# Exact-part value products for the first batch, and a later cut of one block's tokens

## The chip, the core and the metric

The kernel runs on one core of a Trainium2 chip. The core has five engines that work beside each other and are tied by semaphores: TensorE (matmul; PE and PEld in the profile), VectorE (DVE), ScalarE (ACT), GpSimd (POOL) and SyncE (SP), which issues most DMAs. The metric is the device time in microseconds. A time is the median of several executions; a profile is one more execution, recorded instruction by instruction.

## What is computed

An attention with a polynomial sketch, and a SwiGLU feed-forward block on its output. The parts of the reference that matter:

```python
batch, n_heads, seq, head_dim = (4, 4, 1088, 32)     # r = 8
def phi(x):
    a = np.einsum('rd,bhsd->bhsr', S1, x)
    b = np.einsum('rd,bhsd->bhsr', S2, x)
    return np.einsum('bhsi,bhsj->bhsij', a, b).reshape(*x.shape[:-1], r * r)
q_p, k_p = (phi(q), phi(k))
kv = np.einsum('bhsf,bhsd->bhfd', k_p, v)
z = np.sum(k_p, axis=2)
num = np.einsum('bhsf,bhfd->bhsd', q_p, kv)
den = np.einsum('bhsf,bhf->bhs', q_p, z)[..., None] + 1e-06
x = num / den                                        # to (4352, 128)
g = x @ w_gate                                       # d_ff 1536
silu = g * (1.0 / (1.0 + np.exp(-g)))
out = (silu * (x @ w_val)) @ w_out
```

The inputs are float64 and are read as pairs of 32-bit words; the kernel narrows them to float32 itself.

## The kernel before, in words

**Tokens and units.** The 4352 tokens are cut into blocks. Batch 0 (the "first batch", 1088 tokens) is blocks 0, 1 and 2 of 384, 384 and 320 tokens. The rest is seven blocks: 3 to 8 of 480 and 9 of 384. The feed-forward width of 1536 is twelve chunks of 128. A *unit* (i, j) is block i with chunk j: the gate and the value product, silu, and their product, which is one hidden tile in one of a list of `slots`. A *down* product multiplies a hidden tile by a chunk of `wo` and adds it up in a bank of PSUM; after it the slot goes back to the end of the list.

**Two kinds of unit.** `unit` makes both products in float32 (L1015), takes silu on ScalarE (L1019) and multiplies on VectorE straight out of PSUM (L1030). `cut_unit` makes a product from *exact parts*: weights and tokens are each split into a coarse part (w1, x1), a remainder (wb, x0) and a mixed part (wd, xd), each stored as fp32r. One product is then three fp32r matmuls: xd by wd (L968), x1 by w1 (L978) and x0 by wb (L979). ScalarE copies the first out of PSUM (L972), VectorE adds the others to it (L980), and GpSimd multiplies by silu (L991). With `both=False` the gate product stays in float32 (L970); with `both=True` both are made from parts.

**Making parts.** For weights of three chunks: ScalarE makes w1, an engine subtracts (`low`), ScalarE scales it (wb), and the engine makes wd (`cut_weights`, L865). For `wv` the engine is GpSimd, for `wg` VectorE. For tokens of one block (`cut_tokens`): ScalarE makes x1 (L875), GpSimd x0 (L876) and, in a later step, VectorE xd (L880).

**Narrowing.** Each weight piece of three chunks is turned from 64-bit words into float32 by `narrow` in three steps: two masks on VectorE (L256, L257); two activations on ScalarE (L261, L262); two joins on VectorE (L264, L270) and one product on GpSimd (L279).

**Order.** The scheduling is by hand: each engine runs its instructions in the order in which the Python program issues them. In the first-batch loop (L1278) a step z issues one unit of `seq`, then steps of narrowing (`parts`), from z=17 on one down product and one piece of the attention of the next batch (`parts_of`), and between them the parts of `wv`. A `late` unit, of which there are six before the loop, leaves silu and the value product apart, and `catch_up` (L1036) multiplies them on GpSimd later: three ahead of the loop, three at z=24, 25 and 26. After the loop come 23 down products among pieces of the attention, then the main loop over y (84 units of blocks 3 to 9), the first 20 of them with the gate product in float32. In both loops each engine is in order, so an instruction that waits holds up what is behind it.

**The attention of batch 1** runs beside z=17 to 29: kT and qT are transposed on VectorE, key sketches on TensorE (L347), features `phk` on VectorE (L370), sums of features `zs` on GpSimd (L540); then `values` on TensorE: `key_values` (L381) and four products with `zs` (L713), and after them the key sketches of batch 2. `fold` and `spread_out` follow on VectorE (L594 to L723), and the query sketches (L335) need what `fold` writes. `query_step` makes `phT` on VectorE, and `numerators` (L776) uses it. The attention of batch 2 has the same course in the main loop: `values` ahead of y=4, the query sketches ahead of y=6.

**Buffers.** Before, there are 27 slots of 384 columns: 17 in `hbuf` and 10 in `late`. In the main loop `hbuf` is cut anew into 13 slots of 480 columns; `late` holds remainders of the gate weights, later the features of batch 3 and the parts of `wo`. From z=17 on units take turns in three PSUM banks.

The steps z of the first-batch loop and the main loop's y are numbered as in the code; z=12 starts at 41.00 us in the profile, z=18 at 49.38, z=29's unit ends at 76.54, and y=0 starts at 93.06.

Of the kernel before, what the change touches and what calls it, by code (L numbers as in the profile page):

```python
# [19 lines left out]
def kernel(  # L20
# [28 lines left out]
    nc = tc.nc  # L49
# [253 lines left out]
    NH = 27  # L303
    NL = 10
    hbuf = const.tile([P, NH - NL, BW], FP32, name="hbuf")
    late = const.tile([P, NL, BW], FP32, tag="late", name="late", bufs=1)
    slots = [(hbuf[:, k, :] if k < NH - NL else late[:, k - NH + NL, :]) for k in range(NH)]
# [300 lines left out]
    def attentions():  # L608
# [31 lines left out]
        values(kvz[:, 0, :], phk, zs)  # L640
        kab, kcopies = sketched(wide("b"), key_products, 2, "kab2")
        fold(kvz[:, 0, :])
# [23 lines left out]
        for b in (2, 3):  # L666
# [19 lines left out]
            if b == 2:  # L686
                yield from turn_queries(3)
                phk = late[:, NL - 6 :, :].rearrange("p s (n h i j) -> p (s n) h i j", h=1, i=R, j=R)
                phk = phk.rearrange("p (c h) o i j -> p c (h o) i j", h=H)
                yield from features(phk, kab)  # L690
                zs, sums = feature_sums(phk)
# [17 lines left out]
    def values(kv, phk, zs):  # L709

        key_values(kv[:, 0:F], phk, 0, NC)
        for h in range(H):
# [105 lines left out]
    def homes(w):  # L818


        if w is wv:
            for c in range(4):
                yield [
                    stage.tile([P, 3, P], F32R, tag=tag, name=name, bufs=6)[:]
                    for tag, name in (("exp", "w1"), ("man", "wb"), (("exp", "man")[c % 2], "wd"))
                ]
        else:
            big = lambda pool, tag, bufs: pool.tile([P, 2, 3, P], F32R, tag=tag, name="g" + tag, bufs=bufs)
            for c in range(2):
                t = [big(stage, "raw", NRAW), big(stage, "raw", NRAW), big(apool, "phq", 2)]  # L830
                for k in range(2):
                    yield [x[:, k] for x in t]

    def cut_weights(w, lows, engine):

        rows = [], [], [], []
        sub = dict(op=ALU.subtract)
        for c, (w1, wb, wd) in enumerate(homes(w)):
            src = w[:, 3 * c : 3 * c + 3, :]
            low = lows[c]  # L840
            w_parts[id(w), c] = (w1, wb, wd)
            fine = dict(out=wd, in0=whole(w1), in1=whole(wb), **sub), engine.tensor_tensor
            if engine is nc.vector:
                fine = dict(
                    out=wd, in0=low, scalar=-BETA, in1=whole(w1), op0=ALU.mult, op1=ALU.add
                ), engine.scalar_tensor_tensor
            for row, f, args in zip(
                rows,
                (nc.scalar.activation, engine.tensor_tensor, nc.scalar.activation, fine[1]),
                (  # L850
                    dict(out=w1, in_=src, func=AF.Copy, scale=CUT),
                    dict(out=low, in0=src, in1=whole(w1), **sub),
                    dict(out=wb, in_=low, func=AF.Copy, scale=BETA),
                    fine[0],
                ),
            ):
                row.append((f, args))
        return rows

    def take(steps, n):  # L860

        for _ in range(n):
            if steps:
                f, args = steps.pop(0)
                f(**args)  # L865
# [410 lines left out]
    seq += [(i, j) for j0 in (6, 9) for i in range(3) for j in range(j0, j0 + 3)]  # L1276
    order = [(i, j) for i in range(3) for j in range(NCH)]
    for z, (i, j) in enumerate(seq):  # L1278
# [3 lines left out]
        unit(i, j)  # L1282
        for p in parts.get(z, ()):
            part(*p)
        if z in (24, 25, 26):
# [5 lines left out]
        if z >= 17:  # L1291
            todo.remove(order[0])
            todo.insert(0, order.pop(0))
            down()
# [119 lines left out]
```

## Time and profile before

| what | us |
|---|---|
| median of 8 runs (lowest to highest) | 287.17 (286.62 to 288.54) |
| the profiled execution | 286.97 |
| its span, first to last instruction | 285.0 |
| PE busy in 93.06 to 111.06 (18.00) | 16.86 |
| PE busy in 111.06 to 190.00 (78.94) | 78.40 |
| POOL, L991 hidden products x83 | 105.0 |
| DVE, L980 sums x83 | 83.3 |
| ACT, L972 copies x83 | 70.9 |

A span is shorter than the time of its execution by what lies before the first and after the last instruction. A line of a timeline gives start and length in microseconds, engine, line of the code, operation, output and inputs, tile sizes, how often, and in brackets how long the engine had been idle and who ended that. A line of waits gives the waiting engine and line, who released it, the total, how often and the longest. A line of stages gives the stretch, its length, and the busy time of PE, PEld, DVE, ACT and POOL. Lengths of matmuls overlap, so start-to-start times tell their cost. The TensorE clock is 1.00 throughout.

### The profile page before, as it was taken

To read this page: it belongs to the slowest core of one execution; us is meant where nothing else is said; L and a number is where in the kernel's file an instruction comes from. 1 tells how busy PE (TensorE), PEld (TensorE's weight loads), DVE (VectorE), ACT (ScalarE), POOL (GpSimd) and SP (SyncE) were. 2 spreads that over 40 slices of the span, in tenths; PEclk is the share of its full clock that TensorE was granted. 3 is DMA by queue.
4 is the path that set the end of the run, shared out by engine and by line. 5 is a ranking of instruction groups with operands and counts; after the bars stand their busy time and mean duration, and the time that the engine had idled before them with its cause. 6 is when DMAs were issued, how large, how long until landed. Compare 5 with 4: busy or idle time off the path is not lost.

```text
span 285.0 us, 5583 instructions
## 1 busy us (share of the span) xinstructions
PE 277.1 (97%) x2129; PEld 191.3 (67%) x2129; DVE 220.7 (77%) x324; ACT 175.2 (61%) x316; POOL 177.1 (62%) x173
## 2 busy tenths in 40 slices
PE   8899999999999989999999999999999999999995
PEld 7545565666665656555576767657777777778984
DVE  3997988975495968998557898749889969988741
ACT  3567665723401846655366776867878888877760
POOL 3315432279500876589935787759879789878660
PEclk9999999999999999999999999999999999999999
DMA  6574193222311122000200020001000200010021
GB/s 195 160 218 114 55 285 117 81 78 81 92 31 28 26 81 74 21 0 2 33 18 0 0 36 2 0 2 22 13 0 1 37 0 0 10 28 1 0 35 28
DMA packets 26138, 14.28 MB, mean 50 GB/s; under 512 B 19840, under 2 KB 24192, under 8 KB 26112
## 3 DMA queue, kind: packets, MB, share of 16 engines
q1 hardware_dynamic: 25456, 13.84, 18.7%
q8 instruction: 16, 0.26, 0.4%
q10 hardware_dynamic: 656, 0.10, 0.2%
q14 instruction: 10, 0.08, 0.1%
HBM read 11.41 MB, written 2.23 MB: 48 GB/s over the span
## 4 chain that ended last, share of the span: by engine, by line
PE 89%; DVE 5%; ACT 2%; POOL 2%; issue 1%; DVEq 0%; ACTq 0%; POOLq 0%
PE PS L1060 24%; PE PS L1015 16%; PE PS L968 11%; PE PS L978 10%; PE PS L979 10%; PE PS L970 4%; PE PS L776 2%; PE PS L335 2%; PE PS L234 2%; PE PS L347 1%; POOL hbuf L991 1%; PE PS L381 1%; DVE xd L880 1%; PE PS L1088 1%; PE PS L1055 1%
## 5 line engine op out<-in xcount | busy, mean ns | idle before, releaser
L991 POOL TENSOR_TENSOR hbuf<-sg,sum 128x480 f32<-128x480 f32 (+1 forms) x83 | 105.0, 1269 | 37.7 <-ACT sg L986 29.4
L980 DVE SCALAR_TENSOR_TENSOR sum<-PS,sum 128x960 f32<-128x960 f32 (+2 forms) x83 | 83.3, 1003 | 26.7 <-ACT sum L972 21.6
L972 ACT ACTIVATE sum<-PS 128x960 f32<-128x960 f32 (+2 forms) x83 | 70.9, 854 | 39.4 <-PE PS L968 37.9
L1060 PE MATMUL PS<-hbuf,wo 128*128 128x480 f32 (+3 forms) x142 | 57.5, 505 | 0.0
L968 PE MATMUL PS<-xd,gphq 128*128 128x480 f32 (+1 forms) x63 | 40.1, 636 | 0.5 <-DVE xd L880 0.5
L978 PE MATMUL PS<-x,w 128*128 128x480 f32 (+1 forms) x83 | 38.5, 464 | 0.0
L986 ACT ACTIVATE sg<-sum 128x480 f32<-128x480 f32 (+1 forms) x63 | 36.6, 581 | 0.9 <-DVE sum L980 0.9
L968 PE MATMUL PS<-xd,wd 128*128 128x480 f32 (+1 forms) x83 | 35.8, 432 | 0.5 <-DVE xd L880 0.5
L1060 PEld LDWEIGHTS PS<-hbuf,wo 128*128 128x128 f32 x142 | 26.6, 189 | 8.4 <-issue 0.9
L979 PE MATMUL PS<-x,wb 128*128 128x480 f32 (+1 forms) x83 | 31.2, 376 | 0.0
L1015 PE MATMUL PS<-xT,wg 128*128 128x384 f32 (+1 forms) x74 | 29.5, 480 | 0.0
L1015 PE MATMUL PS<-xT,wv 128*128 128x384 f32 (+1 forms) x74 | 28.8, 471 | 0.2 <-DVE wv L279 0.2
L1019 ACT ACTIVATE sg<-PS 128x384 f32<-128x384 f32 (+1 forms) x31 | 14.3, 466 | 21.4 <-PE PS L1015 19.8
L968 PEld LDWEIGHTS PS<-xd,wd 128*128 128x128 f32 x83 | 15.7, 189 | 13.1 <-issue 11.4
L978 PE MATMUL PS<-x,graw 128*128 128x480 f32 (+1 forms) x63 | 23.5, 373 | 0.2 <-ACT xT L793 0.2
L979 PE MATMUL PS<-x,graw 128*128 128x480 f32 (+1 forms) x63 | 23.3, 370 | 0.0
L1060 PE MATMUL PS<-hbuf,scaled 128*128 128x480 f32 x48 | 23.2, 564 | 0.0
L1015 PEld LDWEIGHTS PS<-xT,wv 128*128 128x128 f32 x74 | 13.8, 190 | 9.2 <-DVE hbuf L1030 0.9
L968 PEld LDWEIGHTS PS<-xd,gphq 128*128 128x128 f32 x63 | 11.9, 188 | 11.7 <-issue 6.8
L1015 PEld LDWEIGHTS PS<-xT,wg 128*128 128x128 f32 x74 | 13.3, 189 | 9.3 <-issue 1.2
L978 PEld LDWEIGHTS PS<-x,w 128*128 128x128 f32 x83 | 15.6, 188 | 5.8 <-issue 3.6
L979 PEld LDWEIGHTS PS<-x,wb 128*128 128x128 f32 x83 | 15.6, 188 | 5.7 <-issue 4.3
(173 smaller groups left out, 457.6 us busy)
## 6 DMA issues: line engine op xcount, KB each, us to landing
kld<-in_k_dram SPq DMA_DIRECT2D x4, 544.0 KB, 4.1
vld<-in_v_dram SPq DMA_DIRECT2D x12, 144.0 KB, 4.4
qld<-in_q_dram SPq DMA_DIRECT2D x3, 544.0 KB, 3.4
raw<-in_moe_w_out_dram SPq DMA_DIRECT2D x4, 384.0 KB, 3.8
raw<-in_moe_w_gate_dram SPq DMA_DIRECT2D x3, 384.0 KB, 3.7
raw<-in_moe_w_val_dram SPq DMA_DIRECT2D x3, 384.0 KB, 4.0
out_dram<-o SPq DMA_DIRECT2D x16, 60.0 KB, 1.9
vld<-in_v_dram SPq DMA_DIRECT2D x4, 112.0 KB, 4.3
```

Of the source, the lines that this page charges most:

```text
L234: nc.tensor.matmul(ps[0:32, 0:w], warm[:, 0:32], warm[:, 0:w], start=True, stop=True)
L968: nc.tensor.matmul(ds[:, k], wd, xd, start=True, stop=True)
L970: nc.tensor.matmul(g, wg[:, j, :], xT[:, t0 : t0 + n], start=True, stop=True)
L972: nc.scalar.activation(sums, ds, AF.Copy, scale=-1.0 / BETA)
L978: nc.tensor.matmul(ps[:, k], w1, x1, start=True, stop=False)
L979: nc.tensor.matmul(ps[:, k], wb, x0, start=False, stop=True)
L980: nc.vector.scalar_tensor_tensor(out=sums, in0=ps, scalar=1.0 + 1.0 / BETA, in1=sums, op0=ALU.mult, op1=ALU.add)
L986: nc.scalar.activation(sg, sums[:, 0] if both else g, AF.Silu)
L991: nc.gpsimd.tensor_tensor(out=hj[:, 0:n], in0=sg, in1=sums[:, len(ws) - 1], op=ALU.mult)
L1015: nc.tensor.matmul(o[:, 0:n], w[:, j, :], xT[:, t0 : t0 + n], start=True, stop=True)
L1019: nc.scalar.activation(sg[:, 0:n], g[:, 0:n], AF.Silu)
L1060: nc.tensor.matmul(acc[i][:, 0:n], w, hidden[i, j][:, 0:n], **sides)
```

## The change

It has two parts.

*Part 1.* In the main loop, the parts of block 4 (`line[1]`) are issued in units 3 and 8 instead of 2 and 3: ScalarE's x1 and GpSimd's x0 after y=3, VectorE's xd after y=8. That puts xd behind VectorE's `fold` and `spread` of batch 2's sums and behind five more of the units' sums.

*Part 2.* In the first batch the eighteen units of chunks 6 to 11 are made block by block (all of block 0, then 1, then 2) instead of three chunks at a time. The last twelve of them, z=18 to 29, blocks 1 and 2, become `cut_unit` with the gate in float32 and the value product from parts. For that the parts of `wv` are made in two halves: chunk groups 3 and 2 (chunks 9 to 11 and 6 to 8) at z=11 to 16, groups 0 and 1 at z=20 to 27; tokens of block 1 at z=13 and 15, of block 2 at z=16 and 19. The three late products go from z=24 to 26 to z=8 to 10. In the attention of batch 1 the four products with `zs` move behind the key sketches of batch 2 (`value_sums` apart from `key_values`). There are 24 slots of 384 instead of 27 (14 in `hbuf`, 4 in `late`, 6 in a new tile `more`), 11 slots of 480 in the main loop up to y=20 and 15 from there, instead of 13. The weights' parts get other homes, and `cut_weights` and `take` become a generator `cut_chunk` with the same four instructions.

```diff
-    NH = 27
+    NH = 24
     NL = 10
     hbuf = const.tile([P, NH - NL, BW], FP32, name="hbuf")
-    late = const.tile([P, NL, BW], FP32, tag="late", name="late", bufs=1)
-    slots = [(hbuf[:, k, :] if k < NH - NL else late[:, k - NH + NL, :]) for k in range(NH)]
+    late = const.tile([P, 4, BW], FP32, tag="late", name="late", bufs=1)
+    more = const.tile([P, NL - 4, BW], FP32, name="more")
+    slots = [t[:, k, :] for t, n in ((hbuf, NH - NL), (late, 4), (more, NL - 4)) for k in range(n)]
...
-        values(kvz[:, 0, :], phk, zs)
+        key_values(kvz[:, 0, 0:F], phk, 0, NC)
         kab, kcopies = sketched(wide("b"), key_products, 2, "kab2")
+        value_sums(kvz[:, 0, :], zs)
         fold(kvz[:, 0, :])
...
         if w is wv:
+            x, y = (big(apool, "phq", 2) for _ in range(2))
+            yield 3, [x[:, 0], x[:, 1], y[:, 0]]
+            x = const.tile([P, 3, 3, P], F32R, name="w2")
+            yield 2, [x[:, k] for k in range(3)]
+            yield 0, [exp(), man(), exp()]
+            yield 1, [exp(), man(), man()]
         else:
+            for c in range(NCH // 3):
+                x = big(stage, "raw", NRAW)
+                yield c, [x[:, 0], x[:, 1], (exp, man)[c % 2]()]
...
+    def cut_chunk(w, home, low, engine):
+        c, (w1, wb, wd) = home
+        src = w[:, 3 * c : 3 * c + 3, :]
+        nc.scalar.activation(w1, src, AF.Copy, scale=CUT)
+        yield
+        engine.tensor_tensor(out=low, in0=src, in1=whole(w1), op=ALU.subtract)
+        yield
+        nc.scalar.activation(wb, low, AF.Copy, scale=BETA)
+        yield
...
+            engine.tensor_tensor(out=wd, in0=whole(w1), in1=whole(wb), op=ALU.subtract)
+        w_parts[id(w), c] = w1, wb, wd
+        yield
...
-    seq += [(i, j) for j0 in (6, 9) for i in range(3) for j in range(j0, j0 + 3)]
+    seq += [(i, j) for i in range(3) for j in range(6, NCH)]
...
+        if z == CUTS:
+            turn[0] = 1
+        if z < CUTS:
+            unit(i, j)
+        else:
+            cut_unit(i, j)
...
-        if z in (24, 25, 26):
+        if z in (8, 9, 10):
             catch_up()
...
+        if z == 11:
+            give(cut_chunk(wv, next(home_v), room_for(fpool, "o", 2), nc.gpsimd), 11, 12, 14, 15)
+            give(cut_chunk(wv, next(home_v), room_for(fpool, "o", 2), nc.gpsimd), 12, 13, 15, 16)
+            give(cut_tokens(1), 13, 15)
+            give(cut_tokens(2), 16, 19)
         if z == 20:
+            lows = [room_for(fpool, "o", 2) for _ in range(2)]
+            give(cut_chunk(wv, next(home_v), lows[0], nc.gpsimd), 20, 21, 25, 26)
+            give(cut_chunk(wv, next(home_v), lows[1], nc.gpsimd), 21, 22, 26, 27)
         if z >= 17:
             parts_of(1)
+        for gen in steps_at.get(z, ()):
+            next(gen, None)
...
-        for at in {2: (20, 22), 3: (27, 32), 4: (40, 42)}.get(m, (NCH * m - 10, NCH * m - 9)):
+        for at in {1: (3, 8), 2: (20, 22), 3: (27, 32), 4: (40, 42)}.get(m, (NCH * m - 10, NCH * m - 9)):
...
         if y == GATES:
             hold("g2")
+            slots += wide_slots(more, NL - 4)
```

`CUTS` is 18. The instructions of each engine, in order: up to z=10 as before but for the two catch-up products among them; on GpSimd then the last catch-up product, `low` of chunk groups 3 and 2, x0 of block 1, the product of wo piece 0, wd of group 3, the product of wo piece 1, wd of group 2, x0 of block 2, and from there the hidden products of the units. From y=0 on every engine's order is the one before, apart from the two moved steps of block 4.

## The prediction

> **What bounds the kernel now.** I read the busy shares first, then what TensorE waited for, then the stages, then single engines around the two places that are edited.
>
> ```profile
> PE 277.1 (97%) x2129; PEld 191.3 (67%) x2129; DVE 220.7 (77%) x324; ACT 175.2 (61%) x316; POOL 177.1 (62%) x173
> ```
>
> TensorE works 277.1 of 285.0 us. Its waits, longest in total first:
>
> ```profile
> PE PS L335 <- DVE spread L723: 1.1, 1, 1.1
> PE PS L968 <- DVE xd L880: 1.0, 2, 0.5
> ```
>
> The busy times by stage:
>
> ```profile
> 41.00:49.38 8.38, 8.38 (x27) 4.94 (x26) 6.82 (x17) 4.64 (x11) 2.08 (x3) 1.00 0.52 166
> 49.38:76.54 27.16, 27.16 (x295) 17.95 (x294) 18.04 (x36) 12.19 (x29) 17.70 (x18) 1.00 0.22 69
> ```
>
> After the length the columns are PE, PEld, DVE, ACT and POOL. From 41.00 (step z=12 of the first-batch loop) to 76.54 (end of z=29) TensorE never rests, so work removed there is time gained and any wait added there is time lost. The first stage shows the room that POOL has before z=18: it works 2.08 of 8.38 us. The prices on TensorE, from its timeline (start, length, instruction):
>
> ```profile
> 48.74 0.81 PE L1060 MATMUL PS<-hbuf,wo 128*128 128x384 f32 x2
> 49.38 0.70 PE L1015 MATMUL PS<-xT,wg 128*128 128x320 f32 x2
> 49.92 0.70 PE L1015 MATMUL PS<-xT,wv 128*128 128x320 f32 x2
> ```
> ```profile
> 256.22 0.34 PE L968 MATMUL PS<-xd,wd 128*128 128x384 f32 x1
> 256.39 0.34 PE L978 MATMUL PS<-x,graw 128*128 128x384 f32 x1
> 256.57 0.34 PE L979 MATMUL PS<-x,graw 128*128 128x384 f32 x1
> ```
>
> Starts count, not lengths, since matmuls overlap: a float32 product of 384 columns takes 0.64 us (48.74 to 49.38), one of 320 takes 0.54, a product of exact parts of 384 takes 0.174.
>
> **What the Trainium skill says.** "FP8 and Floating Point Precision", TensorE Precision Notes: true FP32 makes four passes. The trace agrees: 0.64 / 0.174 = 3.7. "SBUF — State Buffer", Who interferes with whom: a VectorE instruction with two SBUF inputs and a GpSimd instruction that reads SBUF exclude each other, and the later one blocks until the first is through. The trace agrees in both directions. On VectorE:
>
> ```profile
> 92.27 0.65 DVE L880 SCALAR_TENSOR_TENSOR xd<-x,x 128x480 fp32r<-128x480 f32 x1
> ...
> 104.29 1.65 DVE L880 SCALAR_TENSOR_TENSOR xd<-x,x 128x480 fp32r<-128x480 f32 x1 [2.27 <-POOL x L876]
> ```
>
> The first met an idle POOL, the second a POOL product from 104.22 to 105.42. On POOL, two hidden-tile products started at 98.90 and 100.08 (1.18 apart), and the next steps, into each of which one such VectorE instruction fell, were 1.49 long: 0.31 each. "Perfetto Trace Analysis", GPSIMD Engine Instruction, advises start-to-start times for GpSimd; they are 0.96 us for a 128x384 product here (26.71, 27.67, 28.62).
>
> **Part 1: the tokens of block 4 in units 3 and 8.** In y=3 VectorE first waits for POOL (2.27 us), then runs xd (1.65), and only then `fold` and `spread` (105.87 to 106.8); TensorE's sketches (L335) wait 1.09 us for that. Moved to y=8, xd leaves `fold` behind the second gate remainder (L865, over at 102.02): s123 is done near 103.1, against 105.76 when TensorE comes. The 1.09 us go. What is late next: ScalarE's copy and POOL's remainder x0 are issued a unit later, behind one more hidden product (1.2 us) with five units to spare. At y=8 xd costs 1.1 us (mean of L880, which includes blocking) to 1.65 where VectorE has no idle time (112 to 122). Queued behind it are the sums of y=9 to 13; that of y=10 started 2 us behind TensorE and would end near 123.2, its bank being reused three units later, near 124. VectorE's small waits from 128 to 134 let it catch up. xd itself is ready near 119.5 and wanted at 121.8. I take -1.0; bounds -1.1 and -0.4 (lost cover at y=10). No DMA moves queue; the shift and load issues of `spread` only go out earlier.
>
> **Part 2: twelve units by exact parts.** The set of shapes from z=18 on is the same before and after (six units of 384, six of 320). *Gain on TensorE:* the value product falls from 0.645 to 3 x 0.174 = 0.522 for 384 (-0.123), from 0.538 to 3 x 0.145 = 0.435 for 320 (-0.103; 0.145 is the 384 step by columns). 6 x 0.123 + 6 x 0.103 = -1.36.
>
> *What ScalarE and VectorE get:* per unit one copy out of PSUM on ScalarE (L972 with 480 columns 0.57) and L980 instead of L1030 on VectorE (0.64 for 480 columns, by columns 0.51 for 384, against 0.55 for L1030: no more). ScalarE worked 12.19 of 27.16 us, so twelve copies of 0.5 fit.
>
> *What POOL gets before z=18.* In program order it now has, after the gate piece at 39.61: three catch-up products (from z=24 to 26 to z=8 to 10), the narrowing of wv piece 4, two `low`, x0 of block 1, wo piece 0, wd of chunk 3, wo piece 1, wd of chunk 2. That wd is the stationary operand of the first matmul of z=18, due at 49.38. From 39.61 these are twelve steps of 0.96: 39.61 + 12 x 0.96 = 51.1, plus 0.1 to pass on. So TensorE stands at least 1.9 us even if nothing blocks. That floor needs no assumption beyond in-order issue. Then the blocking: the same stretch has seven VectorE instructions with two SBUF inputs (L264 and L270 of wv 4, wo 0, wo 1; xd of block 1). At 0.31 each, 7 x 0.31 = 2.2 on POOL. And they come in a chain: L264 of wv 4 (40.60) meets the catch-ups, delaying L270 to about 43.3 and with it wv 4; xd waits for x0 near 48.5, then for POOL's product; L264/L270 of wo 1 come behind xd, and wo 1 behind them, before wd. Walking that queue gives wd of chunk 2 at 54.1 to 54.3, 4.7 us late; with only the 2.2 added, 53.4, 4.0 late. I take 4.4; bounds 1.9 and 5.1. The smaller waits at z=13 and z=17 (late VectorE products, late banks) lie inside it, as TensorE would wait at z=18 anyway.
>
> *What comes after.* From z=18 to `zs` of batch 1 POOL has x0 of block 2 (0.85), seven hidden products (0.96 each; before, z=24's catch-up was the only one), two wo pieces, two `low` and the sums, which took from 62.92 to 68.38:
>
> ```profile
> 62.92 2.49 POOL L540 TENSOR_TENSOR zs<-phk 128x512 f32<-128x512 f32 x2
> 65.49 2.08 POOL L540 TENSOR_TENSOR zs<-zs 128x512 f32<-128x512 f32 x2
> 67.65 0.73 POOL L540 TENSOR_TENSOR zs<-zs,phk 128x256 f32<-128x256 f32 x1
> ```
>
> That is 0.85 + 6.7 + 3.84 + 5.46 = 16.9, plus five blockings (1.6) and some 2.9 idle while the first units are made: 21.4. TensorE reaches `value_sums` after 6 x 1.82 + 3 x 1.62 + 1.28 + 1.13 + 1.22 = 19.4 (units with their down products, first key sketches, values, second key sketches, which the split puts ahead of the sums). Missing: 2.0. Also z=24's exact product needs the one bank that VectorE frees with the sum of z=23, behind three phk products: 0.4 if nothing blocks, up to 1.9 if L264/L270 of wo 3 do; the more is lost there, the less at `zs`. I take +2.3 together; bounds 0.9 and 2.8. At z=28 the DVE chain to phT starts as before; its end (85.2) has 1.3 us before the numerators (86.53), which covers POOL products blocking two or three of its steps (0.3 to 0.5 each).
>
> Slots (14 + 4 + 6 instead of 17 + 10), homes and gate steps keep TensorE's order from y=0 on; cover: the slot taken is freed by a down product that TensorE runs before. Cost nothing; at most one late down, 0.2.
>
> **Sum.** -1.0 - 1.36 + 4.4 + 2.3 = +4.3. On the profiled execution (span 285.0, 286.97 with what lies around it) 291.3; the runs' median 287.17 is 0.2 higher, within their spread (286.62 to 288.54). Forecast 291.2 us.
>
> **Rivals.**
> - *Floor only, 287.7.* POOL's queue is late by its work alone (+1.9) and `zs` by 0.9: -2.36 + 2.8 = +0.4. For it: blocking shows only in a few instructions of this trace. Against: every one that overlaps shows it.
> - *The other side, faster, 285.0.* One mechanism: POOL hands over the wd of chunk 2 in time at z=18, and -2.4 stand (286.97 - 2.4 = 284.6; 285.0 with small waits). It decides if the waits at z=18 and `zs` come to less than 2.4 together. Against: twelve steps of 0.96 from 39.61. For: POOL is only 2.08 us busy in the stage before.
> - *Deeper, 293.2.* The rest of a standing of 4 us turns into a slower TensorE clock: "TensorE: Matmul & The Clock Gate", Part 1, gives half clock after an idle window of about 3.4 us, released after as long, an estimate of up to 1.7 us more; no run here shows it (the clock is 1.00 in all stages). Or the lag outlasts 1.3 us at the numerators.
> - *Part 1 does nothing*: another wait takes L335's place; 292.2, inside the forecast's own range.
>
> **How the numbers follow.** Chances: forecast 0.56 (289.5 to 292.6), floor 0.18, faster 0.08, deeper 0.18. About 0.3% (0.86 us) is what a measurement of this kernel can tell from none. The floor case straddles it (0.08 same, 0.10 slower). So faster 0.08, same 0.08, slower 0.84. Leaving out faster, the lower half of the floor and the top of deeper gives 288.0 to 293.4.
>
> **What would show it.** TensorE idle before the first xd,w product near 49.4, released by POOL's wd, ending near 54 (51.3 for the floor); POOL near full from 40 to 54; L264/L270 near 41 and 47 lengthened from 0.55 to about 1; a wait of the sums (L719) for zs or of L972 for VectorE's sum before z=24; steps of 1.82 us from unit to unit from z=18; no wait of the sketches near y=6. If the first xd,w product starts within 0.5 us of the down product before it, my main term is wrong.

## The result, and the profile after

The kernel after takes 295.74 us (median of 11 runs, 294.89 to 297.29), the one before 287.06 (31 runs, 286.61 to 288.54): 1.0294 times as long, 95% interval 1.0278 to 1.0309. The forecast was 291.2 (288.0 to 293.4). The sign was right, the size a little under half of what came. Of the eleven runs, three kept a mean TensorE clock of 1.000 and took 294.89 to 294.93 us; the other eight, with 0.987 to 0.994, took 295.62 to 297.29, and the profile below is one of these.

The profiled span is 293.9 us. The head of the page (busy time, share, instructions):

```profile
PE 279.3 (95%) x2141; PEld 192.4 (65%) x2141; DVE 227.2 (77%) x326; ACT 181.1 (62%) x330; POOL 191.7 (65%) x187
...
PEclk9999999899999999999999999999999999999999
```

TensorE counts 2.2 us more busy time than before (277.1) though it has less to do. Part of that is the clock, which drops in one slice, the eighth; there the same products take longer. The rest is the way of counting: a product that starts behind a wait doesn't overlap with the one before it (in lows_late, below, the clock stays at 1.00 and the count is still 278.5). What the kernel loses beside the clock is standing still. TensorE's waits, after:

```profile
PE PS L962 <- POOL w L857: 2.8, 1, 2.8
PE PS L972 <- DVE sum L974: 1.7, 2, 1.3
PE PS L962 <- DVE xd L874: 1.0, 2, 0.5
PE PS L719 <- POOL zs L541: 0.9, 1, 0.9
...
PE PS L1009 <- ACT sg L1013: 0.7, 1, 0.7
PE PS L1009 <- DVE more L1024: 0.6, 1, 0.6
PE PS L1009 <- DVE late L1024: 0.6, 1, 0.6
```

L962 is the product xd by wd (L968 before), L972 the first of the two products into the shared bank (978), L1009 the float32 product of `unit` (1015), L719 the product with `zs` (713). All of these but L962's wait for xd (1.0 before too) are new; the sketches' wait of 1.1 us for `spread` is gone. By stages (length; PE, PEld, DVE, ACT, POOL; then the clock):

```profile
41.00:49.40 8.40, 6.48 (x19) 2.86 (x17) 6.38 (x11) 4.25 (x11) 6.64 (x7) 1.00 0.50 163
49.40:55.76 6.36, 3.42 (x10) 1.33 (x8) 5.35 (x10) 2.70 (x7) 4.44 (x6) 1.00 0.00 0
55.76:60.86 5.10, 5.10 (x15) 3.49 (x15) 2.51 (x5) 1.97 (x5) 1.77 (x2) 0.67 0.00 0
60.86:86.71 25.85, 23.28 (x294) 16.67 (x293) 17.79 (x32) 13.84 (x34) 20.52 (x21) 1.00 0.21 69
```

The first row covers the time that z=12 to 17 took before; TensorE now works 6.48 of 8.40 us there, and POOL 6.64 instead of 2.08. z=18's first matmul comes at 55.76 instead of 49.38, and after a standing of 2.8 us the clock is 0.67 for 5.1 us.

The starts of z=12, z=18 and y=0 cut every profile into three stages that can be compared whatever happens ahead of z=12. (It starts between 40.99 and 42.99 us in the profiles below. TensorE's wait for kT near 6 us varies from run to run, up to 1.6 us; in w1_after, banks and combo2 the products right behind it are slower too, 2.0 to 2.2 us for the key sketches of batch 0 instead of 1.49.) In us:

| kernel | z=12 to 18 | z=18 to y=0 | y=0 to end |
|---|---|---|---|
| before | 8.38 | 43.68 | 191.94 |
| after | 14.77 | 47.47 | 190.67 |
| the difference | +6.39 | +3.79 | -1.27 |
| forecast | +4.4 | +0.94 (-1.36 + 2.3) | -1.0 |

So the first two stages hold the error. What holds z=18 up is seen on three engines. Before, the same joins and the product behind them are short, on VectorE and POOL:

```profile
40.60 0.55 DVE L264 SCALAR_TENSOR_TENSOR exp<-raw,exp 128x384 int32<-128x384 int32 x1
41.07 0.55 DVE L270 SCALAR_TENSOR_TENSOR man<-raw,man 128x384 f32<-128x384 uint32 x1
41.70 0.99 POOL L279 TENSOR_TENSOR wv<-man,exp 128x384 f32<-128x384 f32 x1 [1.09 <-DVE man L270]
```

ScalarE after (start, length, instruction, and in brackets the idle time before it and who ended that):

```profile
40.65 0.44 ACT L1013 ACTIVATE sg<-PS 128x320 f32<-128x320 f32 x1 [0.64 <-PE PS L1009]
44.34 0.52 ACT L846 ACTIVATE wphq<-wv 128x384 fp32r<-128x384 f32 x1 [3.26 <-POOL wv L279]
44.77 0.47 ACT L1013 ACTIVATE sg<-PS 128x384 f32<-128x384 f32 x1
```

L846 is w1 of chunk group 3, issued in z=11, so it stands before the silu of z=12. It needs the narrowed piece 4 of `wv`, the silu does not, and ScalarE stands 3.26 us. VectorE after, with the masks (L256, L257) and joins (L264, L270) of the narrowing:

```profile
40.59 1.38 DVE L264 SCALAR_TENSOR_TENSOR exp<-raw,exp 128x384 int32<-128x384 int32 x1
41.89 1.35 DVE L270 SCALAR_TENSOR_TENSOR man<-raw,man 128x384 f32<-128x384 uint32 x1
43.16 0.48 DVE L1024 TENSOR_TENSOR late<-sg,PS 128x320 f32<-128x320 f32 x1
45.28 0.55 DVE L1024 TENSOR_TENSOR more<-sg,PS 128x384 f32<-128x384 f32 x1 [1.64 <-ACT sg L1013]
46.36 1.15 DVE L257 TENSOR_SCALAR man<-raw 128x384 int32<-128x384 int32 x1
48.17 0.35 DVE L257 TENSOR_SCALAR man<-raw 128x384 int32<-128x384 int32 x1
```

And POOL after:

```profile
40.56 2.26 POOL L1030 TENSOR_TENSOR hbuf<-hbuf,sum 128x384 f32<-128x384 f32 x2
43.32 0.99 POOL L279 TENSOR_TENSOR wv<-man,exp 128x384 f32<-128x384 f32 x1 [0.50 <-DVE man L270]
...
48.56 1.00 POOL L870 TENSOR_TENSOR x<-xT,x 128x384 fp32r<-128x384 f32 x1 [1.26 <-ACT x L869]
50.53 1.00 POOL L279 TENSOR_TENSOR wo<-man,exp 128x384 f32<-128x384 f32 x1 [0.96 <-PE PS L1009]
51.49 1.31 POOL L857 TENSOR_TENSOR wphq<-wphq 128x384 fp32r<-128x384 f32 x1
53.76 1.00 POOL L279 TENSOR_TENSOR wo<-man,exp 128x384 f32<-128x384 f32 x1 [0.96 <-DVE man L270]
54.72 0.99 POOL L857 TENSOR_TENSOR w<-w 128x384 fp32r<-128x384 f32 x1
```

Read it as one loop. Two catch-ups on POOL stretch VectorE's two joins (1.38 and 1.35 us; 0.55 alone), so POOL's product for `wv` piece 4 starts at 43.32; ScalarE waits for that, VectorE for ScalarE's silu (1.64), POOL for ScalarE's x1 (1.26) and twice for VectorE's joins (0.96 each; at the first the profile names TensorE, but what the product reads is the join that ended at 50.45). The last line is wd of group 2, for which TensorE stands at z=18. POOL is late not by work alone: from 39.60 to 55.71 its twelve steps take 12.4 us, 0.9 more than 12 x 0.96, and for 3.7 us it stands idle, waiting for engines that it held up itself.

### The profile page after: what moved, and what is told of

Its sections match the earlier page's. It is cut to its first block, busy times and chain, and to the rows that moved or that the text cites. A ratio compares the mean times of both kernels' runs of the same rounds, so it can differ in the third digit from the quotient of the medians.

```text
span 293.9 us, 5655 instructions
## 1 busy us (share of the span) xinstructions
PE 279.3 (95%) x2141; PEld 192.4 (65%) x2141; DVE 227.2 (77%) x326; ACT 181.1 (62%) x330; POOL 191.7 (65%) x187
## 3 DMA queue, kind: packets, MB, share of 16 engines
q1 hardware_dynamic: 25456, 13.84, 18.1%
## 4 chain that ended last, share of the span: by engine, by line
PE 77%; DVE 10%; POOL 5%; DMA 2%; issue 2%; ACT 2%; SPq 0%; DVEq 0%; ACTq 0%; POOLq 0%
PE PS L1054 22%; PE PS L962 11%; PE PS L972 10%; PE PS L973 10%; PE PS L1009 7%; PE PS L964 6%; POOL zs L541 3%; PE PS L782 2%; PE PS L336 2%; DMA kld<-in_k_dram 1%; DVE sum L974 1%; PE PS L348 1%; DVE man L270 1%; DVE man L257 1%; DMA raw<-in_moe_w_out_dram 1%
## 5 line engine op out<-in xcount | busy, mean ns | idle before, releaser
L974 DVE SCALAR_TENSOR_TENSOR sum<-PS,sum 128x960 f32<-128x960 f32 (+4 forms) x95 | 89.4, 941 | 36.5 <-ACT sum L966 21.8
L985 POOL TENSOR_TENSOR hbuf<-sg,sum 128x480 f32<-128x480 f32 (+1 forms) x73 | 91.7, 1261 | 38.1 <-ACT sg L980 24.5
L966 ACT ACTIVATE sum<-PS 128x960 f32<-128x960 f32 (+4 forms) x95 | 76.5, 805 | 52.7 <-PE PS L962 50.8
L1054 PE MATMUL PS<-hbuf,wo 128*128 128x480 f32 (+3 forms) x122 | 50.0, 515 | 0.0
L985 POOL TENSOR_TENSOR more<-sg,sum 128x480 f32<-128x480 f32 (+2 forms) x22 | 25.3, 1152 | 9.1 <-ACT sg L980 5.0
L964 PE MATMUL PS<-xT,wg 128*128 128x480 f32 (+2 forms) x64 | 29.1, 536 | 0.0
L962 PE MATMUL PS<-xd,wexp 128*128 128x480 f32 (+1 forms) x52 | 26.4, 553 | 1.0 <-DVE xd L874 1.0
L1054 PEld LDWEIGHTS PS<-hbuf,wo 128*128 128x128 f32 x122 | 23.0, 191 | 6.2 <-issue 0.4
L962 PE MATMUL PS<-xd,wman 128*128 128x480 f32 (+1 forms) x53 | 27.0, 555 | 0.0
L972 PE MATMUL PS<-x,wraw 128*128 128x480 f32 (+1 forms) x63 | 23.6, 375 | 0.2 <-ACT xT L799 0.2
L973 PE MATMUL PS<-x,wraw 128*128 128x480 f32 (+1 forms) x63 | 23.5, 373 | 0.0
L1009 PE MATMUL PS<-xT,wv 128*128 128x384 f32 (+1 forms) x50 | 20.0, 482 | 1.5 <-DVE more L1024 0.6
L980 ACT ACTIVATE sg<-PS 128x480 f32<-128x480 f32 (+2 forms) x32 | 17.0, 532 | 7.0 <-PE PS L964 6.0
L1009 PE MATMUL PS<-xT,wg 128*128 128x384 f32 (+1 forms) x50 | 20.4, 490 | 0.9 <-ACT sg L1013 0.7
L972 PE MATMUL PS<-x,wexp 128*128 128x480 f32 (+1 forms) x42 | 20.2, 480 | 0.0
L962 PEld LDWEIGHTS PS<-xd,wexp 128*128 128x128 f32 x52 | 9.7, 189 | 10.4 <-issue 7.1
L1054 PE MATMUL PS<-hbuf,scaled 128*128 128x480 f32 x34 | 16.4, 564 | 0.0
L973 PE MATMUL PS<-x,wman 128*128 128x480 f32 (+1 forms) x42 | 15.7, 374 | 0.0
L962 PE MATMUL PS<-xd,w 128*128 128x480 f32 (+2 forms) x27 | 13.0, 481 | 2.8 <-POOL w L857 2.8
L962 PEld LDWEIGHTS PS<-xd,wman 128*128 128x128 f32 x53 | 9.9, 189 | 8.5 <-issue 6.6
```

Of the source, the lines that this page charges most:

```text
L962: nc.tensor.matmul(ds[:, k], wd, xd, start=True, stop=True)
L964: nc.tensor.matmul(g, wg[:, j, :], xT[:, t0 : t0 + n], start=True, stop=True)
L966: nc.scalar.activation(sums, ds, AF.Copy, scale=-1.0 / BETA)
L972: nc.tensor.matmul(ps[:, k], w1, x1, start=True, stop=False)
L973: nc.tensor.matmul(ps[:, k], wb, x0, start=False, stop=True)
L974: nc.vector.scalar_tensor_tensor(out=sums, in0=ps, scalar=1.0 + 1.0 / BETA, in1=sums, op0=ALU.mult, op1=ALU.add)
```

## The experiments

Times are medians; the kernel before beside them took 286.93 to 287.17. Unless a diff says otherwise, the edit is made in the kernel after.

**Each part alone.** `p1_alone`, in the kernel before:

```diff
-        for at in {2: (20, 22), 3: (27, 32), 4: (40, 42)}.get(m, (NCH * m - 10, NCH * m - 9)):
+        for at in {1: (3, 8), 2: (20, 22), 3: (27, 32), 4: (40, 42)}.get(m, (NCH * m - 10, NCH * m - 9)):
```

> The kernel before with only the moved token parts of block 4 (units 3 and 8). My theory: the 1.09 us that TensorE waits for the query sketches ahead of y=6 go and nothing takes their place, so -1.0 to -1.3 us (about 285.9). Rival: xd at y=8, where VectorE has no idle time, delays the sums and gives the gain back: within 0.4 us of before.

`p2_alone` has the opposite edit in the kernel after.

> The changed kernel with the token parts of block 4 back in units 2 and 3. If the two parts add up, it is 1.0 to 1.3 us slower than the changed kernel (about 296.9), and the wait of the query sketches ahead of y=6 is back. Rival: the parts of the first batch have changed the state at y=4, so that the token move is worth less than 0.5 us here.

Part 1 alone: 285.86 us (285.56 to 285.95), ratio 0.9953 (0.9936 to 0.9970), y=0 to the end 190.72. Part 2 alone: 297.14, ratio 1.0348 (1.0314 to 1.0383), y=0 to the end 191.82. The kernel after is 1.4 us faster than part 2 alone, where part 1 alone is worth 1.1: the parts add up within their spread, and part 1 is the whole gain of the third stage.

**When the catch-ups run.** `cu_early`:

```diff
-        if z in (8, 9, 10):
+        if z in (5, 6, 7):
             catch_up()
```

> The changed kernel with its three catch-up products at z=5, 6 and 7, where GpSimd was idle, instead of z=8 to 10. Theory A (a chain: the products delay the narrowing of wv piece 4 on GpSimd, ScalarE's w1 of chunk group 3 waits for that piece and holds up silu, and all later parts are late): ScalarE's wait of 3.3 us falls to below 1.5, TensorE's start of z=18 moves from 55.8 to about 52, the clock stays at 1.00, in all -4 to -5.5 us (290.2 to 291.7). Theory B (only GpSimd's amount of work ahead of z=18 counts): three steps of 0.96 less, z=18 at 52.9, -2.9 us. Theory C (the blocking between VectorE and GpSimd is the main cause and goes wherever the products go): less than -1.5 us.

295.26 us, ratio 1.0285 (1.0242 to 1.0328): z=18 starts 0.53 us earlier (55.23), no more. The stage from z=12 to 18 is 1.66 us shorter (13.11), but TensorE loses 0.93 of that just before z=12, which starts at 42.12. The catch-ups now block other instructions of VectorE, the masks, ahead of the same piece:

```profile
36.12 1.09 DVE L256 TENSOR_SCALAR exp<-raw 128x384 int32<-128x384 int32 x1
37.13 1.15 DVE L257 TENSOR_SCALAR man<-raw 128x384 int32<-128x384 int32 x1
```
```profile
44.09 0.52 ACT L846 ACTIVATE wphq<-wv 128x384 fp32r<-128x384 f32 x1 [2.02 <-POOL wv L279]
```

(VectorE, then ScalarE, of cu_early.) My first theory, that the catch-ups' place makes the lag, fell; the third, that the blocking goes wherever the products go, fits.

**ScalarE's order.** `g3_later` moves all four steps of group 3:

```diff
-            give(cut_chunk(wv, next(home_v), room_for(fpool, "o", 2), nc.gpsimd), 11, 12, 14, 15)
+            give(cut_chunk(wv, next(home_v), room_for(fpool, "o", 2), nc.gpsimd), 14, 15, 17, 18)
```

> The changed kernel with the four steps of chunk group 3 (first needed at z=21) three units later, at z=14, 15, 17 and 18 instead of 11, 12, 14 and 15; nothing else. Theory A (ScalarE's w1 of group 3 stands first in line for wv piece 4 and holds up silu, with it VectorE's products, the masks of wo, the next x1 and so GpSimd): ScalarE's wait for wv piece 4 is gone, wd of group 2 ends near 52 to 53 instead of 55.7, the clock stays at or near 1.00, -3.5 to -5 us (290.7 to 292.2). Theory B (amount of GpSimd work ahead of wd of group 2): one step of 0.96 less, -1 us.

`w1_after` has `12, 12, 14, 15` in that place, which puts one instruction, ScalarE's w1, behind the silu of z=12 and leaves every other engine's order as it was.

> The kernel after, with one instruction moved: ScalarE's w1 of chunk group 3 behind the silu of z=12 instead of ahead of it. Theory A (ScalarE's order holds silu, VectorE's products and so the token parts and GpSimd): silu of z=12 starts near 42.4 instead of 44.77, the wait then falls on the silu of z=13, one unit less deep; z=18's first matmul 0.5 to 1.5 us earlier than 55.76 and the time 294.2 to 295.2. Theory B (GpSimd's own queue sets z=18 whatever ScalarE does): within 0.3 us of 295.7, with only the small waits at z=13 to 17 moved into the one at z=18.

g3_later: 293.59 (ratio 1.0229, 1.0207 to 1.0252), z=12 to 18 in 13.04. w1_after: 294.80 (1.0264, 1.0239 to 1.0290), z=12 to 18 in 13.83. ScalarE of w1_after:

```profile
43.84 0.49 ACT L1013 ACTIVATE sg<-PS 128x384 f32<-128x384 f32 x1 [0.75 <-PE PS L1009]
46.35 0.53 ACT L846 ACTIVATE wphq<-wv 128x384 fp32r<-128x384 f32 x1 [2.03 <-POOL wv L279]
```

z=12 starts at 42.99 in this profile, so its silu now comes 0.85 us after that, instead of 3.78. The standing before w1 shrinks to 2.03 us and meets the next silu. One instruction's place is worth 0.94 us of the stage, the whole group's 1.73. That is theory A in kind, but for g3_later I had put 3.5 to 5 us: the greater part of the 6.39 does not hang on these places.

**All of it moved.** `spread`:

```diff
-        if z in (8, 9, 10):
+        if z in (17, 18, 19):
             catch_up()
...
-        if z == 11:
-            give(cut_chunk(wv, next(home_v), room_for(fpool, "o", 2), nc.gpsimd), 11, 12, 14, 15)
-            give(cut_chunk(wv, next(home_v), room_for(fpool, "o", 2), nc.gpsimd), 12, 13, 15, 16)
-            give(cut_tokens(1), 13, 15)
+        if z == 8:
+            gen3 = cut_chunk(wv, next(home_v), room_for(fpool, "o", 2), nc.gpsimd)
+            give(cut_chunk(wv, next(home_v), room_for(fpool, "o", 2), nc.gpsimd), 8, 9, 11, 12)
+            give(gen3, 13, 14, 16, 17)
+            give(cut_tokens(1), 12, 14)
```

> The changed kernel with all parts that z=18 needs made where GpSimd was idle: group 2 at z=8, 9, 11 and 12 (its wv piece 3 is there by 35.8), tokens of block 1 at z=12 and 14, group 3 at z=13, 14, 16 and 17, the three catch-up products at z=17, 18 and 19. Theory A: no wait in z=12 to 18 over 0.3 us in all, clock 1.00, so the 6.4 us of the first stretch and the 1.5 us of slow clock go; the second stretch keeps its 3.5 us or gets up to 1 more from the catch-up products: 287.5 to 289. Theory B (the blocking follows the work to its new place): more than 2 us of waits remain before z=18, 290 or more.

z=12 to 18 falls to 8.53, what it was before (8.38); yet the time is 292.42, ratio 1.0188 (1.0172 to 1.0203), since z=18 to y=0 grows from 47.47 to 49.22 (and its profile is 0.93 longer from y=0 on, all of it behind TensorE's last products, which start 186.1 us after y=0 as in the kernel after). Theory A holds for the first stage and misses the time. TensorE's waits in spread, and ScalarE's longest near z=18:

```profile
PE PS L972 <- DVE sum L974: 3.2, 3, 1.7
PE PS L964 <- ACT sg L1013: 1.2, 1, 1.2
```
```profile
50.06 0.52 ACT L850 ACTIVATE wphq<-low 128x384 fp32r<-128x384 f32 x1 [2.16 <-POOL low L848]
```

This is wb of group 3, which waits for POOL and stands before a silu that TensorE needs: the same pattern at a new place. Part of what no longer waits before z=18 waits after it. The second stage has costs of its own.

**The clock.** `fill18` gives TensorE 13 small matmuls into an unused bank while it stands:

```diff
         if z == CUTS:
             turn[0] = 1
+            keep_warm(13, ps=PS[:, 6, :])
```

> The changed kernel with 13 small matmuls of ones (512 columns, 0.22 us each, 2.8 us) on an unused PSUM bank between the down product of z=17 and unit z=18, in the time in which TensorE stood idle. They compute nothing that is used. Theory: the idle stretch of 2.96 us is what brought the clock to 0.67 in the 5.1 us after it; kept busy, TensorE stays at 1.00 and z=18 to z=20 take 3.6 us again, -1.3 to -1.7 us. Rival: the clock fell for another reason (the earlier small gaps from 42.9 on), so the reading stays below 0.8 and the time within 0.5 us of the changed kernel.

294.70 (294.63 to 295.01; ratio 1.0263, 1.0236 to 1.0289). The stage before z=18 is unchanged (14.84), z=18 to y=0 takes 46.41 instead of 47.47. Stages of fill18, the stretch that had clock 0.67:

```profile
55.76:60.86 5.10, 5.10 (x20) 3.49 (x20) 3.49 (x7) 3.54 (x8) 2.13 (x3) 1.00 0.01 3
```

The slower clock costs 1.06 us, less than the 1.3 to 1.7 expected. The runs agree: all four of fill18 keep a mean clock of 0.998 to 1.000, and they take what the three runs of the kernel after with clock 1.000 take (294.9). In w1_after, with no filling and a wait of 3.3 us at z=18, the clock read 1.00 behind it too, and the stage took the same 46.43 (in that profile it had fallen earlier, to 0.65 between 5.9 and 10 us).

**The banks, and zs.** TensorE waits twice for a bank at L972, at z=21 and z=24. `banks` gives z=18 to 25 two more banks in turn:

```diff
             turn[0] = 1
+            place.update(x6=6, x7=7)
+            free_banks += ["x6", "x7"]
+        if z == 26:
+            del free_banks[3:]
+            turn[0] = 1
```

> The changed kernel with two more PSUM banks (6 and 7, unused until z=26) in the turn of the units z=18 to 25. Theory: the waits of the exact product at z=21 (0.9 us in all) and z=24 (1.7 us) are waits for one bank that VectorE frees late; with five banks they go, and part of it comes back at the products with zs, since GpSimd is no earlier: zs wait from 0.9 to about 2.5. Net -0.5 to -1.2 us. Rival (VectorE is simply behind and its lag comes out elsewhere): no change within 0.4 us.

Both waits go, though z=25's gate product now waits 0.89 us for VectorE, and the stage still takes 47.38. TensorE reaches the sums with `zs` earlier and waits longer there:

```profile
PE PS L719 <- POOL zs L541: 1.9, 1, 1.9
```

The exact product of z=24 and POOL's steps before `zs` (L985 is a hidden product) show why:

```profile
71.80 0.55 PE L972 MATMUL PS<-x,w 128*128 128x320 f32 x1
```
```profile
74.46 1.01 POOL L985 TENSOR_TENSOR hbuf<-sg,sum 128x384 f32<-128x384 f32 x1
75.42 0.88 POOL L985 TENSOR_TENSOR more<-sg,sum 128x320 f32<-128x320 f32 x1
```

z=18 starts at 57.32 here, so the exact product of z=24 comes 14.5 us after it instead of 16.9. POOL's hidden product of z=24 (75.42) comes 18.1 us after it, 0.1 earlier than in the kernel after, since POOL has worked without a break ahead of it. What TensorE no longer loses at the bank it loses at `zs`.

The time, 298.27 (1.0365, 1.0322 to 1.0408), is no verdict on the edit: its profile starts z=12 1.56 us late, behind the slower key sketches of batch 0 (2.19 us instead of 1.49), and is 1.13 longer from y=0 on, all of it behind TensorE's last products.

`lows_late` takes POOL's work on groups 0 and 1 from before zs:

```diff
-        if z == 20:
+        if z == 25:
             lows = [room_for(fpool, "o", 2) for _ in range(2)]
-            give(cut_chunk(wv, next(home_v), lows[0], nc.gpsimd), 20, 21, 25, 26)
-            give(cut_chunk(wv, next(home_v), lows[1], nc.gpsimd), 21, 22, 26, 27)
+            give(cut_chunk(wv, next(home_v), lows[0], nc.gpsimd), 25, 26, 27, 28)
+            give(cut_chunk(wv, next(home_v), lows[1], nc.gpsimd), 26, 27, 28, 29)
```

> The changed kernel with the steps of chunk groups 0 and 1 (needed only at y=0) at z=25 to 29 instead of 20 to 27, so that two GpSimd subtractions no longer stand between the hidden products of z=21 to 23 and zs. Theory: the wait for zs (0.9 us) goes and the joins L264 and L270 of wo piece 3 are blocked less, so the wait at z=24 shrinks too: -0.9 to -2 us. Rival: zs hangs on the hidden product of z=24, which comes from TensorE and VectorE, not on the queue: -0.3 or less. If the later parts block VectorE ahead of the numerators, a new wait there of up to 1 us.

295.90 (294.22 to 296.83; ratio 1.0302, 1.0261 to 1.0344), no change that the runs can tell (its one run with mean clock 1.000 took 294.22, against 294.9 in the kernel after). In the profile the stage takes 45.77, 0.65 less than the 46.42 of the other two kernels with full clock there. L719 still waits 0.9 us, but zs is ready sooner: L719 starts 22.37 us after z=18 instead of 23.49 in fill18, since TensorE waits only 0.17 us at z=24 instead of 1.31. VectorE's joins beside which the two steps stood take 0.55 us each there, against 0.86 and 1.36 in the kernel after. So the two steps of POOL did count, though not at L719. Except in banks L719 waited 0.8 to 0.9 us in every kernel with cut units up to here. POOL after, with TensorE's side of it:

```profile
72.91 1.01 POOL L985 TENSOR_TENSOR hbuf<-sg,sum 128x384 f32<-128x384 f32 x1
73.96 0.87 POOL L985 TENSOR_TENSOR more<-sg,sum 128x320 f32<-128x320 f32 x1
74.79 2.51 POOL L541 TENSOR_TENSOR zs<-phk 128x512 f32<-128x512 f32 x2
```
```profile
72.64 0.42 PE L972 MATMUL PS<-x,w 128*128 128x320 f32 x1 [1.30 <-DVE sum L974]
80.31 0.32 PE L719 MATMUL PS<-zs,ones 128*32 128x64 f32 x8 [0.85 <-POOL zs L541]
```

zs stands behind the hidden product of z=24 (73.96). That product has two limits which nearly meet here: it needs z=24's exact product (72.64) and VectorE's sum behind it, and POOL is at work without a break from 71.00 until just before it. As long as the first limit holds, zs follows TensorE's z=24 at a fixed distance, and what TensorE loses at z=24 makes the wait at L719 no shorter; where z=24 comes sooner, as in banks, POOL's own queue is the limit. `zs_first` puts zs ahead of that hidden product, and changes no other order:

```diff
             if n == 3:
                 release("a")
+                zs, sums = feature_sums(phk)
+                for f in sums:
+                    f()
             if n % 3 != 1:
                 yield
-        zs, sums = feature_sums(phk)
-        for f in sums:
-            f()
```

> The kernel after, with zs on GpSimd ahead of the hidden product of z=24 instead of behind it. Theory A (the 0.85 us come from this place: the hidden product waits for z=24's exact product on TensorE, so zs follows TensorE at a fixed distance): the wait of L719 goes, -0.8 us, 294.5 to 295.2. Theory B (GpSimd's amount of work sets it): zs starts when the steps before it are done and gains at most one step of 0.87 us, but the hidden products behind it come 5.4 us later and TensorE waits for a slot or a bank instead: 295.5 or more.

The wait of L719 is gone and the stage 0.77 us shorter (46.70), with clock 0.71 in its first 5.1 us. The runs do not confirm it: 295.58 (294.86 to 296.41; ratio 1.0292, 1.0266 to 1.0318). Nor does it tell the two limits apart, since zs now stands behind one step of POOL less. The cleaner test is cuts24_zs below.

**Can part 2 pay?** `combo` is spread with the parts of groups 0 and 1 made after the loop, among the down products, and later places for the rest (lines that differ from spread):

```diff
-        if z in (17, 18, 19):
+        if z in (26, 28, 29):
             catch_up()
...
-            give(gen3, 13, 14, 16, 17)
+            give(gen3, 13, 15, 18, 19)
...
-            give(cut_tokens(2), 16, 19)
+            give(cut_tokens(2), 20, 22)
-        if z == 20:
-            lows = [room_for(fpool, "o", 2) for _ in range(2)]
-            give(cut_chunk(wv, next(home_v), lows[0], nc.gpsimd), 20, 21, 25, 26)
-            give(cut_chunk(wv, next(home_v), lows[1], nc.gpsimd), 21, 22, 26, 27)
...
+    rest = [cut_chunk(wv, next(home_v), room_for(fpool, "o", 2), nc.gpsimd) for _ in range(2)]
...
+        for gen in rest:
+            next(gen, None)
```

> As spread, with still less on GpSimd between z=18 and zs: the three catch-ups at z=26, 28 and 29, the parts of groups 0 and 1 made among the 23 down products after the loop, the steps of group 3 at 13, 15, 18, 19 and block 2's tokens at 20 and 22. Theory A (what part 2 costs is the work that GpSimd gets in a fixed order between z=10 and zs; take that work out of the stretch and the gain of 1.36 us on TensorE shows): 285.0 to 287.5, the wait of L719 for zs under 0.5 us and those of L972 for VectorE's sums under 1.2 together. Theory B (the twelve cut units themselves cost it: seven hidden products on GpSimd before zs, each of which excludes the narrowing and the features on VectorE): 289.0 to 292.0, with L972 and L719 together still waiting 3 us or more.

`cuts24` is the same with `CUTS = 24`, block 2's tokens at 17 and 20, and none of block 1's split.

> As combo, but only the six units of block 2 (z=24 to 29) are cut; block 1's stay plain units with the product on VectorE, and its tokens are not split. The gain on TensorE shrinks to 6 x 0.103 = 0.62 us, and zs is made before the first hidden product. Theory A: 284.9 to 286.2 (part 1 alone 285.86, less 0.62, plus small waits). Theory B (hidden products before zs are the cost): also near that, since there are none; a time of 287 or more would speak against both, for the weights' parts themselves.

Both missed: 295.86 (1.0290, 1.0259 to 1.0322) and 293.93 (1.0227, 1.0189 to 1.0264). The main reason is one wait, the same in both, of a down product (L1054) for a catch-up (L1030), and a lower clock behind it (TensorE's stage in cuts24):

```profile
PE PS L1054 <- POOL hbuf L1030: 3.5, 2, 3.0
```
```profile
83.29:86.88 3.59, 3.59 (x6) 2.04 (x7) 3.49 (x4) 0.52 (x1) 2.96 (x3) 0.56 0.01 1
```

The three down products of that stretch take 3.59 us; at clock 1.00 they take 1.94. The catch-ups, put late, stood on POOL behind hidden products that waited for VectorE, and the down products of block 1 waited for them. (In combo TensorE also waited 1.7 us at z=24 for the xd that I had moved to z=22.) With the catch-ups in earlier places, `combo2`:

```diff
-        if z in (26, 28, 29):
+        if z in (17, 18, 19):
             catch_up()
...
-            give(gen3, 13, 15, 18, 19)
+            give(gen3, 13, 14, 18, 18)
...
-            give(cut_tokens(2), 20, 22)
+            give(cut_tokens(2), 16, 19)
```

> As spread (292.42), with the parts of groups 0 and 1 made among the down products after the loop and group 3's last two steps both after z=18. Against combo the catch-ups are back at z=17, 18, 19 and block 2's tokens at z=16 and 19. If GpSimd's amount of work between z=18 and zs is the cost (theory A), four steps of 0.96 us less there and the 1.17 us for ScalarE's wb give 289.0 to 291.5. If the hidden products in themselves are (theory B), it stays at 292 or above.

`cuts24b`, against cuts24:

```diff
-        if z in (26, 28, 29):
+        if z in (18, 19, 20):
             catch_up()
...
-            give(cut_tokens(2), 17, 20)
+            give(cut_tokens(2), 17, 19)
```

> As cuts24 (293.93), with the catch-ups at z=18, 19, 20, where GpSimd stood idle, instead of z=26, 28, 29, where they stood behind the hidden products and TensorE waited 3.5 us for them and ran at a lower clock after it. If that placing explains its excess, 287.0 to 289.5: less 3.5 and about 1.5 for the clock. Against part 1 alone (285.86), a gain of 0.62 us on TensorE stands against the wait of 0.86 us for zs; under 285.3 would beat it.

combo2: 290.52 (1.0125, 1.0095 to 1.0156), as expected for less work on POOL before zs and the best with all twelve units cut, z=18 to y=0 in 47.95, 1.27 less than spread. cuts24b: 286.94 (0.9995, 0.9984 to 1.0006), 7 us less than cuts24, for the places of the three catch-ups and one token step (in the two profiles the stage from z=18 to y=0 differs by 5.56, the wait and the clock). `cuts24_zs` is cuts24b with the edit of zs_first:

> cuts24b (286.94) with zs ahead of the first hidden product, that of z=24. Theory A: the wait of 0.87 us goes, 286.0 to 286.3. Theory B: 286.8 or more. To beat part 1 alone (285.86) it would need under 285.3.

285.99 us (285.69 to 286.68), ratio 0.9952 (0.9934 to 0.9971): 0.95 less than cuts24b, and TensorE no longer waits at L719. In cuts24b the hidden product ahead of zs found POOL idle:

```profile
65.02 0.87 POOL L985 TENSOR_TENSOR more<-sg,sum 128x320 f32<-128x320 f32 x1 [1.94 <-DVE sum L974]
```

So there it was not POOL's work that held zs, but the product that POOL waited for: theory A, for a kernel without the clock drop. The time equals that of part 1 alone (285.86) and does not beat it: z=18 to y=0 takes 43.60, 0.09 less than there, where six cheaper products should save 0.62. The other half microsecond lies at z=24, whose exact product starts 0.80 us after its gate product (63.56 to 64.36) instead of the 0.29 of z=25; VectorE's product of z=23 had ended just before, at 64.30.

## Why the forecast was right in sign and half in size

- *Part 1, -1.0.* Right: -1.22 in the stage from y=0 of p1_alone, -1.1 in its median. No other wait took L335's place.
- *Gain on TensorE, -1.36.* Not contradicted: where no wait falls the units come as fast as forecast (z=20 1.81 us instead of 1.93, z=25 1.63 instead of 1.73, from the starts in the two traces). The stage never shows it as a sum.
- *Wait for wd of chunk 2, +4.4.* Place, releaser and cause were right; the term measured +6.39. "The smaller waits at z=13 and z=17 lie inside it" does hold for TensorE. What failed is the walk of POOL's queue to 54.1 to 54.3 (it ended at 55.71). I put 2.2 us for blocking on POOL and less than 1 for the chain; measured are 0.9 of blocking on POOL and 3.7 of standing. I walked POOL's queue against VectorE and left ScalarE out: the walk has no term for a ScalarE instruction that waits ahead of a silu, worth 0.94 by w1_after, nor for masks blocked by POOL (1.15 instead of 0.35), which the seven counted instructions leave out. How much the blocked VectorE instructions cost by themselves, no run separates.
- *What comes after, +2.3.* Without the clock's 1.06 the stage is 2.73 over before, so +4.1 where I put +2.3. What failed is the length of POOL's course to `zs`, 21.4. In fill18, with full clock, zs is ready 23.4 us after z=18's start: POOL's steps take 17.4, less than the 18.5 that I counted, but it stands 6.1 us where I put 2.9, waiting for VectorE's sums. TensorE's 19.4 was right (23.49 to L719, less the delays of 1.34, 1.71 and 0.90 at z=21, z=24 and L719, counted from start to start, is 19.5). "The more is lost there, the less at `zs`" holds in banks alone; in lows_late the wait at z=24 falls to 0.17 us and L719 still waits 0.9.
- *Clock.* I left it to a rival (*Deeper*, at most 1.7, chance 0.18). It costs 1.06 in the profile; eight of the eleven runs show a lower mean clock.

By stage that is +1.99 of error before z=18, 1.06 for the clock, 1.8 for the rest of that stage, and 0.27 gained more at the end: 4.6 together, from +4.3 to +8.9 of span. "TensorE: Matmul & The Clock Gate", Part 1, describes the window for the idle time as free-running; that fits a clock that fell after 2.8 us of waiting in one kernel and stayed after 3.3 us in another. Its length of about 3.4 us, which the prediction took over, doesn't fit a fall after 2.8 us, the longest standing there, and the measurement decides. No run measured the window's phase.

Of the rivals, *Floor only* and *faster* fell with z=18 at 55.76, and *Part 1 does nothing* with p1_alone. *Deeper* named both mechanisms that made the difference, clock and lag, though its 293.2 fell short as well and its lag was to come at the numerators, where no wait was seen. spread shows that the standing before z=18 can be removed by moving steps alone (8.53 against 8.38): wd of group 2 is the fourth of POOL's steps from 39.66 on, not the twelfth from 39.61, and the catch-ups, a wo piece and wd of group 3 come after z=18. The "floor" of 1.9 us that I called free of assumptions assumed the order of the change.

Open: combo2 takes 47.95 from z=18 to y=0, where 43.68 less the gain of 1.36 would be 42.32. Its waits at L972 (1.8 and 0.6), L719 (0.8) and L962 for a wd (0.6) make 3.8 of the 5.6 us. Counted from start to start, the delays at these places and two small ones at L972 (z=20 and z=22) come to about 6 us, so nothing of size is lost elsewhere; but no run separates hidden products that block VectorE from hidden products that come late themselves. The best versions found are part 1 alone (285.86) and cuts24_zs (285.99), both below the kernel before and not told apart by these runs.

## What to carry to other kernels

Before new work goes into a strictly ordered queue, list what stands behind it on that engine and who waits for that; do so for every engine that the new work touches, not only the busiest one. A step on an engine with room can cost more than its length if it waits ahead of a short instruction that feeds the critical engine: one ScalarE step behind a silu instead of ahead of it was worth 0.94 us, and three catch-up products and one token step, moved to other places, 7 us with the clock. Where a consumer waits by the same amount in many variants, look also for the instruction of the critical engine that its producer itself hangs on: in cuts24b that was the limit, while in the kernel after the producer's own queue was as late.

## What the runs showed of the hardware

- VectorE's masks (L256, L257), with a single SBUF input, take 0.35 us alone and up to 1.09 and 1.19 beside POOL; "SBUF — State Buffer", Who interferes with whom, names `tensor_scalar` among those that can take the shared ports, and the traces agree. The sums and products that read PSUM kept their length (L974 with 384 columns 0.51 to 0.56) beside the same POOL work.
- After 2.8 us of waiting at z=18 the clock read 0.67 over the next 5.1 us in after and 0.71 in zs_first, but 1.00 in lows_late after the same 2.8 and in w1_after after 3.3. In p2_alone the products right behind the wait ran at full pace for 1.1 us (three starts from 56.05 to 57.15) and were slow after that. 13 small matmuls in the gap kept it at 1.00 in all four runs of fill18. The kernel after had a mean clock of 1.000 in three runs and 0.987 to 0.994 in eight, so whether the clock falls differs from run to run of one kernel.
